# Attention finished by the sixth block, and the first matmul of three blocks as seven half products

## The chip, the core and the metric

The kernel runs on one core of a Trainium2 chip. The metric is device time in microseconds (us) for one execution. Three runs of the kernel before gave 280.96 us as their median (280.19 to 281.14). One execution was profiled; it took 281.67 us, of which the profile covers a span of 279.9 us from the first to the last instruction. The five engines of the core run in parallel, each in the order of its own queue: PE multiplies matrices, DVE and ACT do elementwise work, POOL and SP here mostly issue DMA transfers.

## What is computed

Chunked attention over 8 batches, 8 heads, 576 positions and 64 features, with chunks of 64, and behind it a two-layer block with a swish gate whose steepness is a vector. All tensors are float32; the kernel works in float16 with float32 sums.

```
scores = (q_chunk @ k_chunk.T) / 8          # every chunk of 64 positions by itself
attn   = exp(scores - max) / sum            # softmax over the chunk
x      = attn @ v_chunk                     # to 4608 tokens x 512
h      = x @ w_in                           # 512 -> 2048
g      = h * sigmoid(beta * h)              # beta: one number for each of the 2048
out    = g @ w_out                          # 2048 -> 512
```

## The kernel before

**Units and blocks.** The 4608 tokens are cut into 18 units of 256 tokens; two units make one of nine blocks (j = 0 to 8). Attention is done by unit, the two layers by block of 512 tokens.

**Attention of a unit.** `load_unit` (L120) issues six or more DMAs of q, k and v on POOL's queue, which also turn float32 into float16. From unit 8 on, `emit_T` (L147) issues two DMA transposes of a unit's k and q on SP's queue (`kT`, `qT`), and then asks for the load of the unit four further on; q and k have four buffers each, so that load can start only when the transpose of the unit that used the buffer has landed. `emit_sc` (L205) is 32 small score matmuls and an exp on ACT; `emit_pv` (L239) is 32 small value matmuls; `emit_norm` (L294) divides by the softmax sums on DVE; `emit_xt_dma` (L337) issues two more DMA transposes on SP, which bring the result (`xt`) into the layout that the first layer reads.

**First layer.** `emit_m` (L352) makes one of the 16 groups of 128 hidden features of a block: four matmuls of 128x128 on 512 columns (L359) into one PSUM tile `hps`, a tanh of half of beta times h on ACT (L367), and `emit_mg` (L345), one DVE instruction that makes (tanh + 1) * h (L347) in float16, the tile `gt`. The factor two that this leaves is taken out earlier: the sums of the softmax are made with ones of value 2.0.

**Second layer.** From block 1 on it is done as seven products of half size in place of eight (Strassen's scheme in Winograd's form): `emit_sum` (L412) makes four sums `sm` of quarters of `gt` on DVE, `emit_wt` four of the weights, once; `emit_prod` (L442) is one half of such a product, eight matmuls on 256 columns (L475). Results leave PSUM by an ACT copy (L492) and a DVE add (L495), and go out by DMA from SP (L429).

**Order.** The program is written out by hand. For each block, a list of items with a position between 0 and 1 is sorted, and all engines get their instructions in that order: the 16 groups of block j, the 14 half products of block j - 1, the four sums, and in blocks 2 to 7 the attention of the two units of block j + 1 (L637 to L642). Engines wait for each other by semaphores. PE is in order: a score matmul whose transpose has not landed holds up everything behind it on PE. SP is in order too: the transposes of `xt`, those of k and q and the stores of results share its queue.

Of the kernel before, what the change touches and what calls it, by code (L numbers as in the profile page):

```python
# [15 lines left out]
def kernel(  # L16
# [10 lines left out]
    nc = tc.nc  # L27
# [15 lines left out]
    big = ctx.enter_context(tc.tile_pool(name="big", bufs=1))  # L43
    qk_p = ctx.enter_context(tc.tile_pool(name="qk", bufs=4))
    qt_p = ctx.enter_context(tc.tile_pool(name="qt", bufs=2))
    et_p = ctx.enter_context(tc.tile_pool(name="et", bufs=3))
    rd_p = ctx.enter_context(tc.tile_pool(name="rd", bufs=2))
    x_p = ctx.enter_context(tc.tile_pool(name="x16", bufs=4))
    xt_p = ctx.enter_context(tc.tile_pool(name="xt", bufs=3))
    gt_p = ctx.enter_context(tc.tile_pool(name="gt", bufs=2))  # L50
    sg_p = ctx.enter_context(tc.tile_pool(name="sg", bufs=4))
    osb_p = ctx.enter_context(tc.tile_pool(name="osb", bufs=4))
    osl_p = ctx.enter_context(tc.tile_pool(name="osl", bufs=6))
    ps_p = ctx.enter_context(tc.tile_pool(name="ps_p", bufs=4, space=bass.MemoryType.PSUM))
    ps_s = ctx.enter_context(tc.tile_pool(name="ps_s", bufs=1, space=bass.MemoryType.PSUM))
    ps_x_open = tc.tile_pool(name="ps_x", bufs=1, space=bass.MemoryType.PSUM)
    ps_x = ps_x_open.__enter__()
    ps_y = []

# [6 lines left out]
    braw = const.tile([128, 32], FP32)  # L66
    bt = const.tile([128, 32], FP32)
    w_in16 = [big.tile([128, KDM, 256], FP16, name=f"win{g}") for g in range(8)]
    w_out16 = [big.tile([128, 4, DM], FP16, name=f"wout{g}") for g in range(4)]
    vbig = big.tile([128, NV, H, VP], FP16)  # L70
    wt = [big.tile([128, 8, 256], FP16, name=f"wt{i}") for i in range(4)]
# [3 lines left out]
    NB = len(blocks)  # L75
    XU = 8
    unit_block = {}
    for j, (u0, n) in enumerate(blocks):
# [160 lines left out]
    def emit_pv(u, halves=(0, 1)):  # L239
        et = et_t[u]  # L240
        if u >= XU:
            x = ps_s.tile([128, 2, 512], FP32, tag="s", name="x")
            y = [ps_p.tile([128, 512], FP32, tag="p", name="xe") for _ in range(2)]
            x_t[u] = (x[:, :, 0:7 * (D + 1)].rearrange("p r (n d) -> p r n d", n=7), y)
            for n in (7, 0, 1, 2, 3, 4, 5, 6):
                for r in range(2):
                    s, g = divmod(n, 4)
                    i = 2 * u + s
                    o = x_t[u][0][:, r, n] if n < 7 else y[r][:, 0:D + 1]
                    for c in range(2):  # L250
                        nc.tensor.matmul(  # L251
                            out=o[64 * c:64 * c + 64],
                            lhsT=et[64 * r:64 * r + 64, g % 2, 4 * s + 2 * c + g // 2, :],
                            rhs=vbig[64 * r:64 * r + 64, i % NV, 4 * c + g, 0:D + 1],
                        )
            return
        for s in halves:
            i = 2 * u + s
            pool, tag = (ps_x, "x") if s == 0 else (ps_s, "s")
            x = pool.tile([128, 2, 4, 128], FP32, tag=tag, name="x")  # L260
            for g in range(4):
                for r in range(2):
                    for c in range(2):
                        nc.tensor.matmul(
                            out=x[64 * c:64 * c + 64, r, g, 0:D + 1],
                            lhsT=et[64 * r:64 * r + 64, s, 4 * c + g, :],
                            rhs=vbig[64 * r:64 * r + 64, i % NV, 4 * c + g, 0:D + 1],
                        )
            x_t[u, s] = x
# [6 lines left out]
    def emit_norm_whole(u, s):  # L276
        x, y = x_t[u][0:2]
        if s == 0:
            rx = rd_p.tile([128, 2, 8, 1], FP32, tag="rx", name="rx")
            x16 = x_p.tile([128, 2, 2, 4, D], FP16, tag="x32", name="x16", bufs=2)  # L280
            for r in range(2):
                nc.vector.reciprocal(out=rx[:, r, 7], in_=y[r][:, D:D + 1])
                nc.vector.tensor_scalar(out=x16[:, 1, r, 3], in0=y[r][:, 0:D], scalar1=rx[:, r, 7], scalar2=None,
                                        op0=ALU.mult)
            nc.vector.reciprocal(out=rx[:, :, 0:7], in_=x[:, :, :, D:D + 1])
            norm_part(x16[:, 0], x[:, :, 0:4], rx[:, :, 0:4])
            x_t[u] = (x, rx, x16)
            x16_t[u, 0] = x16[:, 0]
            return
# [25 lines left out]
    def emit_xt_pe(u, s):  # L315
        xf = x16_t.pop((u, s)).rearrange("p r h d -> p (r h d)")
        xp = ps_p.tile([128, 4, 128], FP16, tag="p", name="xp")
        xt = xt_at(u, s)
# [25 lines left out]

    def emit_mg(j, m):  # L345
        c0, n, sg, hps = mg_t.pop((j, m))
        nc.vector.scalar_tensor_tensor(  # L347
            out=gt_t[j][:, m, c0:c0 + n], in0=sg[:, 0:n], scalar=1.0, in1=hps[:, 0:n],
            op0=ALU.add, op1=ALU.mult,
        )  # L350

    def emit_m(j, m, c0=0, n=None, gate=True):  # L352
        n = blocks[j][1] * UNIT if n is None else n
        if j not in gt_t:
            gt_t[j] = gt_p.tile([128, KFF, 512], FP16, tag="gt", name="gt")
        hps = ps_p.tile([128, 512], FP32, tag="p", name="hps")
        xr = xt_t[j].rearrange("p t (r k) (c q) -> p (t r) (k c) q", r=2, c=2)
        for kk in range(KDM):
# [6 lines left out]
            )  # L365
        sg = sg_p.tile([128, 512], FP32, tag="sg", name="sg")
        nc.scalar.activation(out=sg[:, 0:n], in_=hps[:, 0:n], func=ACTF.Tanh, scale=bt[:, m:m + 1])  # L367
        mg_t[j, m] = (c0, n, sg, hps)
# [5 lines left out]
    def emit_t(j, t, k0=0, k1=None):  # L374
        k1 = KFF if k1 is None else k1
        if k0 == 0:
            ops_t[j, t] = ps_p.tile([128, DM], FP32, tag="p", name="ops")
        ops = ops_t[j, t]
# [33 lines left out]
    def emit_sum(j, i, lo=0, hi=8):  # L412
# [6 lines left out]
        nc.vector.tensor_tensor(out=sm[i][:, lo:hi, :], in0=a, in1=b, op=op)  # L419

    acc_t = {}
    oq_t = {}
# [19 lines left out]
    def emit_prod(j, p, t):  # L442
        last = j == NB - 1
        if p == 1 and t == 0:
            if j == 1:
                a = [ps_p.tile([128, 512], FP32, tag="p", name="acc") for _ in range(2)]
            else:
                a = [ps_y[0].tile([128, 512], FP32, tag=n, name=n) for n in ("ya", "yb")]
            if last:
                a = [(a[i], ps_p.tile([128, 512], FP32, tag="p", name="acc")) for i in range(2)]  # L450
            acc_t[j] = a
# [47 lines left out]
    def emit_idle(n, w):  # L499
        d = ps_p.tile([128, 512], FP32, tag="p", name="warm")  # L500
        for _ in range(n):
            nc.tensor.matmul(out=d[:, 0:w], lhsT=idle[:, 0:128], rhs=idle[:, 0:w])

    with tc.manual_schedule():
# [61 lines left out]
        for s in range(4):  # L566
            for t in range(4):
# [12 lines left out]
                if s == 3 and t == 3:  # L580
                    emit_xt_unit(2)
                emit_t(0, t, 4 * s, 4 * s + 4)
        emit_sc(3, True)
        for m in range(2):
# [15 lines left out]
        def att_items(u, a0, w):  # L600
            if u >= XU:
# [5 lines left out]
                    (a0 + (0.70 if u + 1 < XU else 0.10) * w, 3, ("T", u + 1))]  # L607

        for j in range(1, NB):
            if j == 3:  # L610
                ps_x_open.__exit__(None, None, None)
                ps_y.append(ctx.enter_context(tc.tile_pool(name="ps_y", bufs=1, space=bass.MemoryType.PSUM)))
            items = []
# [6 lines left out]
            else:  # L620
                m0 = 0.36 if j == 2 else 0.02
                items += [(m0 + (1 - m0) * m / KFF, 0, ("m", m)) for m in range(KFF)]
                for i, p in enumerate((1, 2, 6, 5, 7, 3, 4)):
                    for t in range(2):
                        items.append((0.98 * (2 * i + t) / 14, 1, ("prod", p, t)))
                if j == NB - 1:
                    for i, c in ((2, 0.74), (0, 0.82), (1, 0.86), (3, 0.90)):
                        items.append((c, 4, ("pre", i)))
                for i in range(4):
                    s0 = (0.01, 0.08, 0.25, 0.33)[i] if j == 2 else 0.005 + 0.07 * i  # L630
                    items.append((s0, 4, ("sum", i)))
                if j == 2:
# [3 lines left out]
                              (0.24, 3, ("T", 6)), (0.30, 2, ("xp", 5, 0)), (0.32, 2, ("xp", 5, 1))]  # L636
                if j + 1 < NB:  # L637
                    if j == 2:
                        items += att_items(6, 0.36, 0.27) + att_items(7, 0.60, 0.27)
                    else:  # L640
                        for i in range(2):
                            items += att_items(2 * j + 2 + i, 0.03 + 0.43 * i, 0.43)  # L642
            items.sort(key=lambda it: it[:2])
            for _, _, it in items:
# [20 lines left out]
                elif it[0] == "wt":  # L665
                    emit_wt(it[1], (1,))
                elif it[0] == "Th":
                    emit_T(it[1], (it[2],))
                elif it[1] < NU:
                    emit_T(it[1])  # L670
        for i in (0, 1, 3):
            emit_sum(NB - 1, i, 4, 8)
        for p in (1, 2, 6, 5, 7, 3, 4):
            for t in range(2):
# [32 lines left out]
```

## Time and profile before

| part of the profiled execution | what it shows |
|---|---|
| whole execution, and its span | 281.67 us, 279.9 us |
| PE busy | 269.3 us, 96% of the span |
| DVE busy, ACT busy | 197.9 us, 147.7 us |
| chain that ended last, share on PE | 84% |
| blocks 3 to 7, each | 27.96 to 27.97 us |
| block 8 (no attention in it) | 26.04 us |
| last 14 half products and the end | 15.65 us |

Busy time is the sum over an engine's instructions. The chain that ended last is followed back from the last instruction, at each step to what released it, so an engine with 84% of that chain is the one that sets the time. The blocks are read as the stretches between the first half products of consecutive blocks; block 3 runs from 98.38 to 126.35 us.

### The profile page before, as it was taken

Reading aid. Unit: us, or ns where it says so; the run is one execution under the profiler, and the core shown is the slowest. Engines: PE = TensorE matmul, PEld = TensorE weight load, DVE = VectorE, ACT = ScalarE, POOL = GpSimd, SP = SyncE. Lnnn points to the kernel's source line nnn. Section 1 sums busy time; section 2 is a strip of 40 time slices with the busy share of each in tenths; the row PEclk is TensorE's granted clock in tenths of the full one; section 3 lists DMA queues with packets and bytes.
Section 4 is the critical chain, followed back from the end, with each engine's and each line's share of the span. In section 5 each row is a group of like instructions: output and inputs, shape, how many; then the busy total and the mean of one; then the engine's idle time right before and its main releaser. Section 6 shows DMA issues by size and latency. Waiting matters only on the chain.

```text
span 279.9 us, 7409 instructions
## 1 busy us (share of the span) xinstructions
PE 269.3 (96%) x3090; PEld 174.4 (62%) x3090; DVE 197.9 (71%) x357; ACT 147.7 (53%) x234; POOL 97.0 (35%) x124
## 2 busy tenths in 40 slices
PE   7589999899999999999999999999999999999995
PEld 2466445666755566666666666666666666666784
DVE  3557664699987679576957695769576957775841
ACT  3368606886655564546454645464546454544521
POOL 8864478489548805134181525000000000000000
PEclk9959999999999999999999999999999999999999
DMA  9999999999999998999999999991747114111213
GB/s 137 170 196 204 185 174 170 250 171 156 161 139 126 152 215 91 172 166 155 108 136 132 215 107 158 124 190 37 115 115 115 33 44 115 37 40 37 75 40 112
DMA packets 145952, 36.92 MB, mean 132 GB/s; under 512 B 130048, under 2 KB 145408, under 8 KB 145920
## 3 DMA queue, kind: packets, MB, share of 16 engines
q0 software_dynamic: 101216, 18.10, 83.7%
q1 hardware_dynamic: 44704, 18.37, 35.8%
q8 instruction: 24, 0.39, 0.6%
q14 instruction: 8, 0.07, 0.1%
HBM read 36.71 MB, written 9.44 MB: 165 GB/s over the span
## 4 chain that ended last, share of the span: by engine, by line
PE 84%; DVE 6%; POOL 3%; DMA 2%; ACT 2%; issue 1%; DVEq 0%; ACTq 0%; POOLq 0%
PE hps L359 40%; PE ya L475 17%; PE yb L475 12%; PE acc L475 6%; PE ops L380 5%; DVE gt L347 3%; DMA win<-in_moe_w_in_dram 2%; PE sc L214 1%; POOL vbig L115 1%; PE sc L227 1%; ACT sg L367 1%; PE xp L320 1%; PE x L251 1%; DVE x L304 1%; DVE kT L159 1%
## 5 line engine op out<-in xcount | busy, mean ns | idle before, releaser
L367 ACT ACTIVATE sg<-hps,bt 128x512 f32<-128x512 f32 (+1 forms) x158 | 101.8, 650 | 92.5 <-PE hps L359 76.9
L359 PE MATMUL hps<-xt,win 128*128 128x512 f16 (+1 forms) x632 | 145.4, 366 | 1.6 <-DMA win<-in_moe_w_in_dram 0.9
L347 DVE SCALAR_TENSOR_TENSOR gt<-sg,hps 128x512 f16<-128x512 f32 (+1 forms) x158 | 99.1, 636 | 57.5 <-ACT sg L367 57.0
L359 PEld LDWEIGHTS <-win 128*128 128x128 f16 x632 | 61.4, 99 | 44.2 <-issue 1.4
L475 PEld LDWEIGHTS <-sm 128*128 128x128 f16 x512 | 49.0, 98 | 15.3
L475 PEld LDWEIGHTS <-gt 128*128 128x128 f16 x384 | 36.9, 98 | 12.0
L115 POOL DMA_DIRECT2D vbig<-in_v_dram x40 | 34.2, 880 | 10.3 <-DMA wout<-in_moe_w_out_dram 4.3
L101 POOL DMA_DIRECT2D qu<-in_q_dram x22 | 18.6, 859 | 54.8 <-DMA qT<-qu 46.7
L475 PE MATMUL ya<-wt,sm 128*128 128x256 f16 x208 | 27.0, 273 | 0.0
L419 DVE TENSOR_TENSOR sm<-gt 128x2048 f16<-128x2048 f16 (+1 forms) x17 | 19.6, 1156 | 0.3
L101 POOL DMA_DIRECT2D ku<-in_k_dram x22 | 18.8, 881 | 0.0
L380 PE MATMUL ops<-wout,gt 128*128 128x512 f16 x64 | 14.5, 380 | 0.0
L475 PE MATMUL ya<-wout,gt 128*128 128x256 f16 x104 | 13.5, 273 | 0.0
L475 PE MATMUL yb<-wt,sm 128*128 128x256 f16 x104 | 13.5, 273 | 0.0
L475 PE MATMUL yb<-wout,gt 128*128 128x256 f16 x104 | 13.5, 273 | 0.0
L475 PE MATMUL yb<-wout,sm 128*128 128x256 f16 x104 | 13.5, 273 | 0.0
L475 PE MATMUL ya<-wt,gt 128*128 128x256 f16 x104 | 13.5, 273 | 0.0
L236 ACT ACTIVATE et<-sc 128x1024 f16<-128x1024 f32 (+1 forms) x9 | 7.3, 833 | 11.5 <-PE sc L227 11.5
L272 DVE TENSOR_TENSOR x<-x,rx 128x512 f16<-128x512 f32 (+1 forms) x20 | 12.4, 620 | 0.3
L492 ACT COPY osb<-ya 128x512 f32<-128x512 f32 x18 | 10.6, 587 | 2.4 <-PE ya L475 2.4
L304 DVE TENSOR_TENSOR x<-x,rd 128x512 f16<-128x512 f32 (+1 forms) x20 | 11.3, 583 | 0.6
L380 PEld LDWEIGHTS <-gt 128*128 128x128 f16 x64 | 6.0, 98 | 6.9
(69 smaller groups left out, 203.0 us busy)
## 6 DMA issues: line engine op xcount, KB each, us to landing
out_dram<-osb SPq DMA_DIRECT2D x32, 256.0 KB, 3.9
vbig<-in_v_dram POOLq DMA_DIRECT2D x32, 128.0 KB, 7.7
qu<-in_q_dram POOLq DMA_DIRECT2D x20, 128.0 KB, 5.7
ku<-in_k_dram POOLq DMA_DIRECT2D x20, 128.0 KB, 7.0
win<-in_moe_w_in_dram POOLq DMA_DIRECT2D x8, 256.0 KB, 9.4
wout<-in_moe_w_out_dram POOLq DMA_DIRECT2D x4, 512.0 KB, 12.8
qu<-in_q_dram POOLq DMA_DIRECT2D x4, 256.0 KB, 6.7
ku<-in_k_dram POOLq DMA_DIRECT2D x4, 256.0 KB, 6.2
```

The costliest lines, as they stand in the source:

```text
L101: nc.gpsimd.dma_start(out=tv[off:off + n, sp], in_=src[b, :, s:s + n, :].rearrange("h p d -> p h d"),)
L115: nc.gpsimd.dma_start(out=vbig[off:off + n, i % NV, :, 0:D], in_=v[b, :, s:s + n, :].rearrange("h p d -> p h d"),)
L236: nc.scalar.activation(out=et[:, s], in_=sc[:, s], func=ACTF.Exp, scale=scale)
L272: nc.vector.tensor_tensor(out=x16, in0=x[:, :, :, 0:D], in1=rd.to_broadcast(list(x16.shape)), op=ALU.mult)
L304: nc.vector.tensor_tensor(out=o, in0=x[:, r, :, 0:D], in1=rd[:, r].to_broadcast(list(o.shape)), op=ALU.mult)
L347: nc.vector.scalar_tensor_tensor(out=gt_t[j][:, m, c0:c0 + n], in0=sg[:, 0:n], scalar=1.0, in1=hps[:, 0:n], op0=ALU.add, op1=ALU.mult,)
L359: nc.tensor.matmul(out=hps[:, 0:n], lhsT=w_in16[m // 2][:, kk, (m % 2) * 128:(m % 2) * 128 + 128], rhs=xr[:, c0 // CH:(c0 + n) // CH, 2 * ...
L367: nc.scalar.activation(out=sg[:, 0:n], in_=hps[:, 0:n], func=ACTF.Tanh, scale=bt[:, m:m + 1])
L380: nc.tensor.matmul(out=ops, lhsT=gt_t[j][:, kk, t * 128:(t + 1) * 128], rhs=w_out16[kk // 4][:, kk % 4, :], start=(kk == 0), stop=(kk == K ...
L419: nc.vector.tensor_tensor(out=sm[i][:, lo:hi, :], in0=a, in1=b, op=op)
L475: nc.tensor.matmul(out=dst, lhsT=lhsT, rhs=rhs, start=(p in (1, 2, 5) and kk == 0 and (t == 0 or last)), stop=(kk == 7 and (t == 1 or last ...
L492: nc.scalar.copy(out=o, in_=acc)
```

## The change

Seven parts, all in one edit:

1. Attention is moved ahead. In block 3 three units are done (8, 9, 10), in block 4 four (11 to 14), in block 5 three (15 to 17); blocks 6 and 7 have none. `xt` gets a fourth buffer. The loads keep their rule: four units ahead.
2. From block 6 on (`QB`), groups 4 to 15 of the first layer are made in three sets of four, each as seven half products of 128x128 on 256 columns (`emit_q_prod`), 28 matmuls on 256 columns for 16 on 512. Groups 0 to 3 stay as they were.
3. The seven products need four sums of weights for each set (`emit_ws`, 12 DVE instructions, in block 6) and four differences of `xt` for each block (`emit_tx`, 4 DVE instructions).
4. The results of a set are put together by three ACT copies out of PSUM and three DVE adds into a float32 tile `hq`, and gated by six Silu instructions on ACT and four DVE scalings into `gt`. The gate in these blocks is Silu of beta times h, times 1 / beta, for groups 0 to 3 as well; before the block loop `emit_beta` makes both vectors with five small DVE instructions.
5. PSUM pools are closed and opened anew at block 6: two buffers in place of four for `hps`, two each for the new accumulators `qx` and `qz`. The SBUF of attention's tiles is given to the new tiles at position 0.70 of block 5.
6. In the normalisation of units 8 and on, two small DVE multiplications become ACT instructions with a scale.
7. In the last block the first two half products are put between the half products of the first layer, and one sum is made whole after them.

```diff
+    QB = 6
+    QM = (1, 2, 3)
...
-                nc.vector.tensor_scalar(out=x16[:, 1, r, 3], in0=y[r][:, 0:D], scalar1=rx[:, r, 7], scalar2=None,
-                                        op0=ALU.mult)
+                nc.scalar.activation(out=x16[:, 1, r, 3], in_=y[r][:, 0:D], func=ACTF.Copy, scale=rx[:, r, 7])
...
     def emit_mg(j, m):
+        if j >= QB:
+            nc.vector.tensor_scalar(out=gt_t[j][:, m, :], in0=mg_t.pop((j, m)), scalar1=rb[:, m:m + 1], scalar2=None,
+                                    op0=ALU.mult)
+            return
...
+        if j >= QB:
+            nc.scalar.activation(out=sg, in_=hps, func=ACTF.Silu, scale=bs[:, m:m + 1])
+            mg_t[j, m] = sg
+            return
...
+    def emit_ws(i, n):
...
+        in0, in1, op = ((a21, a22, ALU.add), (o[0], a11, ALU.subtract),
+                        (a11, a21, ALU.subtract), (a12, o[1], ALU.subtract))[n]
+        nc.vector.tensor_tensor(out=o[n], in0=in0, in1=in1, op=op)
...
+    def emit_tx(j, n):
...
+        in0, in1 = ((b12, b11), (b22, tx[0]), (b22, b12), (b21, tx[1]))[n]
+        nc.vector.tensor_tensor(out=tx[n], in0=in0, in1=in1, op=ALU.subtract)
...
+    def emit_q_prod(j, i, p):
+        x, z = qz_t[j, i][0:2]
+        dst = x if p in (1, 6, 7, 4) else z
...
+        for s in range(2):
+            for kk in range(2):
...
+                nc.tensor.matmul(
+                    out=dst[:, s, :], lhsT=lhsT, rhs=rhs,
+                    start=(p in (1, 2, 5) and s == 0 and kk == 0),
...
+    def emit_q(j, i, s):
...
+        for p in ((1, 2), (6, 5), (7, 3), (4,))[s]:
+            emit_q_prod(j, i, p)
+            if p in (1, 6, 5):
+                o = {1: hq[:, 0:2, 0], 6: hq[:, 0:2, 1], 5: hq[:, 2:4, 1]}[p]
+                nc.scalar.copy(out=o, in_=z if p == 5 else x)
+            if p in (2, 7, 3):
+                o = {2: hq[:, 0:2, 0], 7: hq[:, 2:4, 1], 3: hq[:, 0:2, 1]}[p]
+                nc.vector.tensor_tensor(out=o, in0=x if p == 7 else z, in1=o, op=ALU.add)
...
+    def emit_q_silu(j, i, part):
...
+        for b in (0, 1):
+            if part == 0:
+                silu(hq[:, 2 + b, 0], x[:, b], 2 + b)
+            elif part == 1:
+                silu(hq[:, b], hq[:, b], b)
+            else:
+                silu(hq[:, 2 + b, 1], hq[:, 2 + b, 1], 2 + b)
...
+    def emit_q_scale(j, i, r):
...
+            nc.vector.tensor_scalar(
+                out=gt_t[j][:, m, :], in0=hq[:, b].rearrange("p c q -> p (c q)"),
+                scalar1=rb[:, m:m + 1], scalar2=None, op0=ALU.mult)
...
+        ATT = {2: ((6, 0.36, 0.27), (7, 0.60, 0.27)),
+               3: ((8, 0.02, 0.33), (9, 0.35, 0.33), (10, 0.68, 0.32)),
+               4: ((11, 0.01, 0.25), (12, 0.26, 0.25), (13, 0.51, 0.25), (14, 0.76, 0.25)),
+               5: ((15, 0.02, 0.27), (16, 0.29, 0.27), (17, 0.56, 0.27))}
+        LANE = [(("m", 0), ("q", 1, 0), ("m", 1), ("q", 1, 1), ("q", 2, 0), ("q", 1, 2), ("q", 2, 1), ("q", 1, 3),
+                 ("q", 2, 2), ("q", 3, 0), ("q", 2, 3), ("q", 3, 1), ("m", 2), ("q", 3, 2), ("m", 3), ("q", 3, 3)),
...
-                if j + 1 < NB:
-                    if j == 2:
-                        items += att_items(6, 0.36, 0.27) + att_items(7, 0.60, 0.27)
-                    else:
-                        for i in range(2):
-                            items += att_items(2 * j + 2 + i, 0.03 + 0.43 * i, 0.43)
+                if j == QB - 1:
+                    items.append((0.70, 6, ("open",)))
+                    items += [(0.72 + 0.04 * n, 6, ("tx", QB, n)) for n in range(4)]
+                for u, a0, w in ATT.get(j, ()):
+                    items += att_items(u, a0, w)
```

## The prediction

> **What bounds the kernel now.** I read the page first (busy shares, slices, chain), then the stretches of the blocks, then the queue of SP with each transpose's landing.
>
> ```profile
> PE 269.3 (96%) x3090; PEld 174.4 (62%) x3090; DVE 197.9 (71%) x357; ACT 147.7 (53%) x234; POOL 97.0 (35%) x124
> ...
> DMA  9999999999999998999999999991747114111213
> ...
> PE 84%; DVE 6%; POOL 3%; DMA 2%; ACT 2%; issue 1%; DVEq 0%; ACTq 0%; POOLq 0%
> ```
>
> PE sets the time; the DMA engines are full until about slice 27 (189 us), which so far costs nothing. Blocks 3, 7 and 8 (columns: stretch, length, then busy time of PE, weight loads, DVE, ACT, POOL; clock, DMA share, GB/s):
>
> ```profile
> 98.38:126.35 27.97, 27.97 (x306) 18.19 (x305) 21.42 (x38) 14.94 (x22) 7.99 (x10) 1.00 1.42 161
> ...
> 210.25:238.21 27.96, 27.96 (x306) 18.18 (x305) 20.84 (x37) 14.95 (x22) 0.00 (x0) 1.00 0.37 77
> 238.21:264.25 26.04, 26.04 (x179) 17.17 (x177) 19.34 (x27) 13.34 (x20) 0.00 (x0) 1.00 0.12 41
> ```
>
> PE has no gap in any block. Block 8 is 14 half products and 16 groups; in the chain a half product is 0.87 us (eight matmuls on 256 columns, 0.109 each), so a group is (26.04 - 12.18) / 16 = 0.866. Two units of attention add 27.97 - 26.04 = 1.93: 0.48 for each step of scores or of values.
>
> **Half products (gain).** Twelve groups are 10.39 us; their 84 matmuls on 256 columns at 0.109 are 9.13. Three blocks: 3 x 1.26 = 3.8 us less, and a block of 24.8 us. Attention's PE work only moves.
>
> **Attention ahead (the cost I hold for decisive).** SP's queue around unit 10's transposes (start, length), then what POOL's next load waits for:
>
> ```profile
> 108.35 2.85 SPq L339 DMA_TRANSPOSE xt<-x  x2
> 111.25 0.57 SPq L429 DMA_DIRECT2D out_dram<-osb  x1
> 111.99 1.46 SPq L154 DMA_TRANSPOSE kT<-ku  x1
> 113.56 4.03 SPq L154 DMA_TRANSPOSE qT<-qu  x1
> ...
> 123.62 1.75 POOL L101 DMA_DIRECT2D qu<-in_q_dram  x2 [10.43 <-DMA qT<-qu]
> ```
>
> This `qT` took 9.5 us from issue to landing; with loads in flight the five from unit 10 on took 9.5, 10.0, 10.3, 9.5, 11.8; after the last load (unit 15 on) 4.2, 4.2, 3.9. Unit 8's took 6.2, issued just as a load began.
>
> In program order the transposes of unit u+1 stand on SP behind the `xt` of unit u-1. From the first value matmul of u-1 to its `xt` the trace has 4.35 us (104.00 to 108.35) or 3.2 (116.25 to 119.45); `xt` to the next instruction 2.9; a store, where one stands between, 0.74; `kT` to `qT` 1.57. So unit u+1 is ready 8.4 to 9.55 us (with a store) or 7.7 to 8.8 (without), plus the landing, after the values of u-1 begin. Before, two units were 12 to 16 us apart and this just fitted; now the pitch is about 9.6 us in block 3 and 7.5 in block 4.
>
> Laying the changed order out with 0.87, 0.866 and 0.48 from 98.38: values of unit 8 at 102.3, scores of 10 at 118.5; values of 10 at 122.5, scores of 12 at 135.2; values of 12 at 138.3, scores of 14 at 151.0. With a landing of 9.5: unit 10 is ready at 120.2 to 121.4 (1.7 to 2.9 late), unit 12 at 140.4 to 141.5 (5.2 to 6.3 late), unit 14, counted from its own stretch, 4.5 to 5.6 late. Together 11.4 to 14.8 us. With 4.2: 0 to 1.3. Odd units follow in the shade of the even ones. Unit 16 has no load beside it: ready 12.6 to 13.8 after the values of 14, scores due 12.7 after them, 0 to 1.1 late, which I leave to the bounds. By capacity instead: a load starts every 14.6 us (107.93 to 166.28 in four steps), of which some 4 us show a DMA share under 1.3 (down to 0.2) where the rest has 1.3 to 2.4; a unit's load, transposes and stores are then about 11 us of work. Five of them from 107.4, where unit 9's `qT` landed, end at 162.4, and up to 4 us of the last load may trail unit 14: 7 to 11 late at 151.0. I take 7, the low end of that and near the middle of 0 to 14.8.
>
> Behind a waiting score matmul on PE stand the half products and groups of the same block; ACT, DVE and the stores wait for those. The load of unit u+4 is late with the transpose, so the lateness doesn't build up loads but spaces them.
>
> **A stall and the clock.** The trace has one such gap (columns as above, the clock is the third from the end):
>
> ```profile
> 10.00:13.10 3.10, 1.10 (x13) 0.75 (x12) 2.38 (x6) 1.45 (x4) 3.10 (x5) 1.00 1.82 181
> 13.10:14.90 1.80, 1.56 (x72) 1.30 (x72) 0.00 (x0) 0.98 (x3) 0.73 (x2) 0.98 1.93 178
> 14.90:21.70 6.80, 6.14 (x63) 4.43 (x62) 4.03 (x12) 3.83 (x9) 3.90 (x7) 0.50 1.45 197
> ```
>
> PE was busy for 1.10 of 3.1 us and then got half the clock for 6.8, a loss of up to 3.4. Two stalls of 5 us could bring that twice, but while PE is slow the transposes catch up, so a stall's second half is partly paid already. Bounds 0 and 6.8; I take 1.7, half of one.
>
> The Trainium skill ("TensorE: Matmul & The Clock Gate", "HAM oscillation — how this bites in real kernels") speaks against this change: a gap longer than one window of about 3.4 us halves the clock, until as long a stretch of work restores it. By it the two longer stalls would cost some 1.7 each, an estimate from that page, 3.4 where I put 1.7; the row above is dearer for one gap.
>
> **DVE in the new blocks.** Adds into `hq` look like L495's (0.682, the same shape and types), sums are 1.218, `tx` and `ws` are half of L410's 0.674 and a bit, 0.41 by the slope to 1.218. The scaling (float32 in SBUF to float16, 128x512) isn't in the trace: the cast of that shape took 0.384, the gate that reads PSUM 0.683. I take 0.42, by the cast, which reads and writes the same memories. A block: 9 x 0.682 + 4 x 1.218 + 3 x 0.682 + 4 x 0.41 + 16 x 0.42 = 21.4 of 24.8 us. Block 6 has 12 `ws` more: 26.3, 1.5 over; half is made up where PE doesn't need it yet: 0.7 (0 to 1.5). At 0.683: 30.5 and 25.6, that is 5.7 + 0.8 + 0.8 = 7.3 over.
>
> **ACT in the new blocks.** Per set three copies of 0.587, two Silu on 512 and four on 256 columns, priced as tanh (0.687, 0.475), 5.0; with 4 x 0.687 and 4 x 0.587 a block has 20.2 of 24.8 us. One more table load (1.28 in the trace) is hidden in the 4.6 left; without that cover it is 1.3. Silu dearer than tanh: 0 to 1 per block, covered too.
>
> **The rest.** Two DVE multiplications of 0.284 a unit go to ACT (0.37 by the 256-column copy, an upper bound), which has 13 us free a block: nothing on the path; if ACT were full, 0.75 a unit. `tx` of block 6 waits on DVE for the last `xt` transposes (2.4 to landing, 1.2 of it behind other work): gates queue behind it, PSUM has four buffers of 0.87 and more: nothing, bound 1.2. `emit_beta` falls where DVE is idle (47 to 50 us): nothing, bound 0.9. Pools anew at block 6: nothing, bound 0.9, one group. At the end, the last half product is followed by two Silu (0.95), two scalings (0.84), two sums (1.38) and some 0.2 of handing over, 3.4, against three half products of PE work (2.6): 0.8 (0 to 1.5).
>
> **Sum.** 281.67 - 3.8 + 7 + 1.7 + 0.7 + 0.8 = 288.1. The profiled execution lies 0.71 over the median of the runs: 287.4.
>
> **Rivals.** *The transposes keep up* (the other side): SP issues them before the load they would collide with, and a `qT` of units 10, 12 and 14 lands within 6 us, as unit 8's did. For it: DMA had idle stretches before. Against: five of five were slow. Stall 0.5: 281.67 - 3.8 + 0.5 + 0.7 + 0.8 = 279.9, by the median 279.2. It decides up to about 2.3 us of stalls in all.
> *DVE becomes the bound* in blocks 6 to 8, scaling at 0.683, transposes in time: 281.67 - 3.8 + 0.5 + 7.3 + 0.8 = 286.5, 285.8 by the median. Against: the cast's row.
> *The half products don't do what they say*: each of the 21 steps a block waits for its accumulator to be copied or added, at 0.11 us, what a half product takes longer behind attention (0.98 for 0.87): 3 x 21 x 0.11 = 6.9, so 281.67 + 3.1 + 0.5 + 0.7 + 0.8 = 286.8, 286.1 by the median. For it: products 6, 5, 7, 3 and 4 all read after a copy or an add. Against: 2.6 us lie between the steps of a set, a copy and an add are 1.3.
>
> **Chances.** Forecast 0.56, transposes keep up 0.28, DVE 0.08, half products 0.08. A measurement here can tell 0.3%, 0.84 us: faster is under 280.1, slower over 281.8. Of the 0.28, 0.25 are faster and 0.03 same; of the forecast 0.04 are same and 0.02 faster (stalls of 2 us); the others are slower. Faster 0.27, same 0.07, slower 0.66. Range: low end the second case less a little, 278.4; high end 294.0, stalls of 11.4 and the clock at 3.4 (281.67 - 3.8 + 11.4 + 3.4 + 1.5 - 0.71 = 293.5). The likeliest case alone has 282 to 294.
>
> **What would show it.** Right: PE waits at L214's scores for `qT` in blocks 3 and 4, chiefly for units 12 and 14, landings of 8 us and over there, blocks 3 to 5 longer than 28.9, 29.9 and 28.9 us, perhaps a clock under 1.00 behind them; blocks 6 to 8 near 25 us. Wrong: blocks 3 to 5 at those lengths with no such wait; or blocks 6 to 8 over 27.

## The result, and the profile after

The changed kernel takes 295.77 us (median of four runs, 295.46 to 295.98) where the kernel before, run beside it, takes 280.85: a ratio of 1.0534, with a 95% interval from 1.0513 to 1.0555. The forecast was 287.4 us with a range up to 294.0: slower as foretold, but by 14.9 us instead of 6.6, and outside the range. The profiled execution took 295.46 us, with a span of 293.7. Ratios here and below leave out a run that took over 1.5% longer than the fastest of its kernel; medians and ranges are of all runs.

The page of the changed kernel, in the lines that were read before: busy time, the granted clock and the DMA engines in 40 slices (7.3 us each), and the chain of waits by engine.

```profile
PE 272.5 (93%) x3198; PEld 186.9 (64%) x3198; DVE 209.1 (71%) x392; ACT 168.0 (57%) x300; POOL 97.0 (33%) x124
...
PEclk9899999999999999799799599999999999999999
DMA  9999999999999999999999966714102011110223
...
PE 64%; DMA 13%; DVE 8%; POOL 5%; ACT 3%; issue 3%; SPq 2%; POOLq 0%; ACTq 0%
```

DMA had 2% of the chain and has 13%. The clock row has three notches (slices 17, 20 and 23) that were not there. They come right behind three waits of PE:

```profile
PE sc L216 <- DMA qT<-qu: 10.4, 3, 3.8
```

That is 10.4 us in three waits, the longest 3.8, all of score matmuls for `qT`. The stretches of these waits and of the work behind each show the two halves of the loss, waiting and a lower clock (columns: stretch, length, then busy time of PE, weight loads, DVE, ACT, POOL; clock, DMA share, GB/s). The last two rows are blocks 6 and 7.

```profile
117.20:120.75 3.55, 0.01 (x3) 0.04 (x2) 1.06 (x2) 0.69 (x1) 0.00 (x0) 1.00 1.37 143
120.75:125.40 4.65, 4.65 (x48) 2.55 (x49) 0.69 (x1) 1.71 (x2) 4.25 (x5) 0.63 1.28 206
...
139.18:142.19 3.01, 0.01 (x2) 0.04 (x2) 3.01 (x4) 0.00 (x0) 0.00 (x0) 1.00 1.13 162
142.19:146.00 3.81, 3.81 (x45) 2.26 (x46) 0.78 (x2) 1.71 (x2) 3.42 (x4) 0.55 0.96 148
...
159.67:163.51 3.84, 0.00 (x0) 0.03 (x1) 0.69 (x1) 0.69 (x1) 0.00 (x0) 0.90 1.75 157
163.51:169.50 5.99, 5.99 (x64) 3.56 (x68) 1.38 (x2) 1.71 (x2) 0.00 (x0) 0.50 1.19 176
...
200.60:226.30 25.70, 25.70 (x218) 21.13 (x216) 23.79 (x46) 17.48 (x32) 0.00 (x0) 1.00 0.14 47
226.30:251.50 25.20, 25.02 (x214) 20.75 (x212) 20.48 (x36) 17.71 (x36) 0.00 (x0) 1.00 0.13 42
```

PE stands for 3.55, 3.01 and 3.84 us, ahead of units 10, 12 and 14; behind each wait it has about half the clock (0.63, 0.55 and 0.50 as the mean of the stretch), which costs 4.65 x 0.37 + 3.81 x 0.45 + 5.99 x 0.50 = 1.7 + 1.7 + 3.0 = 6.4 us. Together 16.8. Blocks 6 and 7 took 25.7 and 25.2 us where 24.8 was forecast.

SP's queue in front of the third wait (start, length of the issue):

```profile
149.48 2.50 SPq L340 DMA_TRANSPOSE xt<-x  x2
152.16 2.46 SPq L156 DMA_TRANSPOSE kT<-ku  x1
154.72 2.35 SPq L156 DMA_TRANSPOSE qT<-qu  x1
```

Unit 12's scores ended at 142.8, its `xt` transposes could be issued at 149.48, unit 14's transposes behind them, and `qT` landed at 163.4, 8.7 us after its issue: 21.4 us from one even unit to the next, where PE had work for 16 (15.8 between the same scores in the run without late loads, below). Unit 17's load was issued from 151.6 to 156.9, into this landing. That suggests two causes, both named in the prediction: the order on SP, and DMA engines that can't move five loads so soon. The experiments take them apart.

### The profile page after: what moved, and what is told of

It is laid out like the page before. It is cut to its first block, busy times and chain, and to the rows that moved or that the text cites. A ratio compares the mean times of both kernels' runs of the same rounds, so it can differ in the third digit from the quotient of the medians.

```text
span 293.7 us, 7739 instructions
## 1 busy us (share of the span) xinstructions
PE 272.5 (93%) x3198; PEld 186.9 (64%) x3198; DVE 209.1 (71%) x392; ACT 168.0 (57%) x300; POOL 97.0 (33%) x124
## 2 busy tenths in 40 slices
DMA packets 145955, 36.95 MB, mean 126 GB/s; under 512 B 130048, under 2 KB 145408, under 8 KB 145920
## 4 chain that ended last, share of the span: by engine, by line
PE 64%; DMA 13%; DVE 8%; POOL 5%; ACT 3%; issue 3%; SPq 2%; POOLq 0%; ACTq 0%
PE hps L364 21%; PE ya L577 12%; PE yb L577 10%; DMA qT<-qu 7%; PE acc L577 5%; PE qx L477 4%; PE qz L477 4%; PE ops L389 4%; DMA qu<-in_q_dram 3%; DMA ku<-in_k_dram 2%; DVE gt L352 2%; POOL vbig L117 2%; ACT hq L505 2%; DVE gt L519 1%; SPq L156 1%
## 5 line engine op out<-in xcount | busy, mean ns | idle before, releaser
L364 PE MATMUL hps<-xt,win 128*128 128x512 f16 (+1 forms) x488 | 110.1, 363 | 1.0 <-ACT xt L325 0.6
L352 DVE SCALAR_TENSOR_TENSOR gt<-sg,hps 128x512 f16<-128x512 f32 (+1 forms) x110 | 67.0, 616 | 45.6 <-ACT sg L376 44.9
L376 ACT ACTIVATE sg<-hps,bt 128x512 f32<-128x512 f32 (+1 forms) x110 | 69.0, 634 | 44.0 <-PE hps L364 43.6
L364 PEld LDWEIGHTS <-win 128*128 128x128 f16 x488 | 47.0, 99 | 34.4 <-issue 3.4
L577 PEld LDWEIGHTS <-gt 128*128 128x128 f16 x384 | 37.3, 99 | 11.3 <-DVE gt L519 1.1
L519 DVE TENSOR_SCALAR gt<-hq,rb 128x512 f16<-128x512 f32 x36 | 15.9, 481 | 7.7 <-ACT hq L505 6.9
L505 ACT ACTIVATE hq<-hq,bs 128x256 f32<-128x256 f32 (+1 forms) x36 | 19.2, 613 | 0.0
L222 ACT ACTIVATE et<-sc 128x1024 f16<-128x1024 f32 x10 | 10.2, 1021 | 12.3 <-PE sc L216 12.3
L477 PEld LDWEIGHTS <-ws 128*128 128x128 f16 x144 | 14.1, 98 | 2.3 <-issue 0.7
L216 PE MATMUL sc<-qT,kT 64*64 64x64 f16 x320 | 4.8, 203 | 10.4 <-DMA qT<-qu 10.4
L495 ACT COPY hq<-qx 128x512 f32<-128x512 f32 x18 | 10.6, 587 | 5.8 <-PE qx L477 5.8
```

Source lines behind the costliest of these rows:

```text
L352: nc.vector.scalar_tensor_tensor(out=gt_t[j][:, m, c0:c0 + n], in0=sg[:, 0:n], scalar=1.0, in1=hps[:, 0:n], op0=ALU.add, op1=ALU.mult,)
L364: nc.tensor.matmul(out=hps[:, 0:n], lhsT=w_in16[m // 2][:, kk, (m % 2) * 128:(m % 2) * 128 + 128], rhs=xr[:, c0 // CH:(c0 + n) // CH, 2 * ...
L477: nc.tensor.matmul(out=dst[:, s, :], lhsT=lhsT, rhs=rhs, start=(p in (1, 2, 5) and s == 0 and kk == 0), stop=(s == 1 and kk == 1), skip_gr ...
L495: nc.scalar.copy(out=o, in_=z if p == 5 else x)
L505: nc.scalar.activation(out=o, in_=src, func=ACTF.Silu, scale=bs[:, m:m + 1])
L519: nc.vector.tensor_scalar(out=gt_t[j][:, m, :], in0=hq[:, b].rearrange("p c q -> p (c q)"), scalar1=rb[:, m:m + 1], scalar2=None, op0=ALU. ...
```

## The experiments

Ratios are against the kernel before, run beside them on the same chip. Its median was 280.42 us beside the first four runs (attention alone, transposes first, no late loads, 16 matmuls on zeros at three places), 281.32 beside the next four (no late v, half the packets, 30 matmuls on zeros, the first slower pace) and 280.65 beside the last four. Differences from the changed kernel's 295.77 cross these rounds, so some 0.5 us of them is uncertain.

**The attention ahead alone.** The kernel before with `xt` bufs 4 and

```
-   items += att_items(2 * j + 2 + i, 0.03 + 0.43 * i, 0.43)
+   for u, a0, w in ATT.get(j, ()):
+       items += att_items(u, a0, w)
```

> The kernel before, with only the attention of units 8 to 17 moved ahead into blocks 3 to 5 (and a fourth xt buffer); no half products, tanh gate throughout. Theory (stalls on the transposes and the half clock behind them are the whole loss): the three gaps of after (3.55, 3.01, 3.84 us) and the clock lost behind them (4.65 x 0.37, 3.81 x 0.45 and 5.99 x 0.50 = 6.4 us) come back here, 16.8 us: 280.9 + 16.8 = about 297.5 us. Rival (part of the loss comes from the second part of the change, its pools and its tail): 285 to 294 us.

297.43 us (296.2 to 298.99), ratio 1.0607 (1.056 to 1.0655). PE waits at the scores of the same units, for 3.4, 2.7 and 4.2 us. The whole loss is in the moved attention. Against this run the rest of the change wins 1.7 us by the medians, 2.1 by the ratios.

**Transposes first on SP.** In `att_items`, for units from 8 on:

```
-   (a0 + 0.10 * w, 3, ("T", u + 1))
+   (a0, 3, ("T", u + 2))
```

(unit 9's transposes come directly behind unit 8's, in block 2).

> The changed kernel, with the q and k transposes of unit u+2 emitted right after the scores of unit u, so that on SP's queue they stand ahead of the xt transposes of unit u instead of behind those of unit u+1's predecessor. Theory (SP's order makes them late; 10 us of landing is then in the shade): qT of units 10, 12 and 14 is issued 9 us or more sooner, no gap of PE over 1 us in blocks 3 to 5, clock 1.00, about 278 to 280 us. Rival (capacity of the DMA engines: loads, transposes and stores of a unit are 11 us of work and the pitch of block 4 is 7.5): landings grow over 12 us, gaps stay at units 13 and 14, 287 to 293 us.

289.9 us (289.37 to 290.98), ratio 1.0349 (1.0317 to 1.038): 5.9 us come back, 9 to 11 don't. This is nearer the rival's case: its time and its waits came, its landings of over 12 us did not. About 1.5 of the rest are of this run's own making: the first groups of block 3 wait 1.3 us, which a later run without unit 9's early transposes does not show. Lines of the transposes from 100 us on (issue time min/median/max in ns, then from issue to landing in us):

```profile
L156 SPq DMA_TRANSPOSE kT<-ku x8: 1242/2654/3730, 101.1 to 176.5; - x8
L156 SPq DMA_TRANSPOSE qT<-qu x8: 1375/2929/3871, 102.4 to 177.9; - x8
...
DMA to landing us min/median/max: 4.4/9.5/10.8
```

`qT` of units 10, 12 and 14 was issued 6.6 to 8.7 us sooner than in the changed kernel (9 expected), but half of the transposes take 9.5 us and more to land, and SP itself is held 2.7 to 2.9 us by an issue. Its queue is nearly full: from 110.4 to 171.4 us its issues take 58.0 of 61.0 us. Four that follow each other:

```profile
144.59 3.45 SPq L156 DMA_TRANSPOSE kT<-ku  x1
148.14 2.23 SPq L156 DMA_TRANSPOSE qT<-qu  x1
150.47 0.54 SPq L531 DMA_DIRECT2D out_dram<-osb  x1
151.10 4.64 SPq L340 DMA_TRANSPOSE xt<-x  x2
```

Waits of 2.4, 2.0, 2.0 and 0.3 us remain at units 13 to 16, and from unit 12 to 15 scores come 11.2, 10.9 and 10.0 us apart: about the pace that the prediction's "11 us of work" for a unit allows. Whether the engines set it directly, or by holding SP's issues, this run doesn't separate.

**No late loads.** In the loads of a unit, where `held` keeps each unit's q and k tiles (`load_v` is left out for these units too, so they compute on older data and give another output):

```
+   if u >= 13:
+       q_t[u], k_t[u] = held[u - 4]
+       held[u] = held[u - 4]
+       return
```

> The changed kernel without the loads of q, k and v for units 13 to 17 (these units compute on data of units loaded before, so the output of those rows is another); every transpose stays. Theory (a transpose lands late because casting loads are in flight): qT lands in about 4 us from unit 10 on, and as SP's order then leaves 0 to 1.3 us of lateness, gaps are under 1.5 us in all, 278 to 280 us. Rival (the order on SP alone makes them late, landing hardly matters): gaps of 2 us and more stay at units 12 and 14, 286 us and over.

279.48 us (278.5 to 280.53), ratio 0.9959 (0.9937 to 0.9981). No score matmul waits any more, with SP's order as in the changed kernel. The transposes from 100 us on:

```profile
L165 SPq DMA_TRANSPOSE qT<-qu x9: 1244/1322/4130, 96.1 to 166.6; - x9
L165 SPq DMA_TRANSPOSE kT<-ku x8: 1232/1269/1291, 108.7 to 165.3; - x8
...
DMA to landing us min/median/max: 3.1/3.3/11.2
```

They land in 3.3 us (median) instead of 9.5, with issues of 1.3 instead of 2.7 to 2.9. The cleaner comparison is with the changed kernel, which has the same order on SP: there `qT` of units 10 to 14 landed in 10.7, 3.3, 8.3, 7.4 and 8.7 us, here in 3.1 or 3.2. (The 11.2 is unit 9's, with unit 12's load still beside it.) So a transpose is slow because loads are in flight beside it. That agrees with the Trainium skill ("DMA: Bandwidth & Descriptors", "SWDGE vs HWDGE vs iDMA"): GpSimd's and SP's transfers share the same 16 engines, which take turns between their queues.

This run also gives the schedule that the changed kernel would have had without the waits. The exponentials of units 10, 12 and 14, which start as the scores end, in the changed kernel:

```profile
121.25 1.02 ACT L222 ACTIVATE et<-sc 128x1024 f16<-128x1024 f32 x1 [3.25 <-PE sc L216]
...
142.84 1.02 ACT L222 ACTIVATE et<-sc 128x1024 f16<-128x1024 f32 x1 [3.75 <-PE sc L216]
...
164.20 1.02 ACT L222 ACTIVATE et<-sc 128x1024 f16<-128x1024 f32 x1 [3.75 <-PE sc L216]
```

and without late loads:

```profile
118.19 1.02 ACT L231 ACTIVATE et<-sc 128x1024 f16<-128x1024 f32 x1
...
134.63 1.02 ACT L231 ACTIVATE et<-sc 128x1024 f16<-128x1024 f32 x1 [0.53 <-PE sc L225]
...
150.69 1.02 ACT L231 ACTIVATE et<-sc 128x1024 f16<-128x1024 f32 x1
```

Its unit 8 came 0.3 us later than the changed kernel's (99.71 and 99.41), so the lateness is 121.25 - 117.9 = 3.4 us at unit 10, 142.84 - 134.3 = 8.5 at unit 12, 164.20 - 150.4 = 13.8 at unit 14. With the 3.0 us of half clock behind unit 14 that is 16.8; the two profiled executions differ by 295.46 - 279.09 = 16.4.

**A third of the late loads less.** `load_v` only for units under 13 (the later ones use older values of v and give another output).

> The changed kernel without the loads of v for units 13 to 17 (a third of the late loads in bytes and in packets; these units use older values, so the output of those rows is another). What is left open by the runs so far: with the transposes moved ahead on SP, units 13 to 16 still came 10.0 to 11.2 us apart, as they did in the changed kernel (21.5 us for two). Theory C (capacity: about 11 us of DMA work a unit, some 7 of it loads): a unit takes about 8.7 us, the scores of unit 14 are 4 to 6 us late instead of 13.5, 284 to 288 us. Rival (fixed latency: a transpose behind any load lands in about 9 us): the gaps stay as they were, 293 us and over.

283.82 us (282.21 to 285.35), ratio 1.0109 (1.0044 to 1.0175), a little under the capacity theory's range. The profiled run, one of the faster two of four (282.42), has waits at units 10, 12 and 13 of 2.0, 1.0 and 1.1 us, the clock at 1.00 throughout, 17.2 us from unit 12 to 14 (8.6 a unit, 8.7 expected) and unit 14's scores 4.2 us late (4 to 6 expected). The transposes' median landing is 5.0 us, so a fixed landing time is out.

**The same bytes in half the packets.** The loads of q and k for units from 13 on by the form that the first eight units use:

```
-   if u >= XU:
+   if XU <= u < 13:
```

> The changed kernel with the loads of q and k for units 13 to 17 in rows of two heads' positions, 512 bytes each instead of 256: the same bytes, half the packets, so a third less of all late packets (the rows stand in another order, so the output of those rows is another). If the packets are what costs: like the run without v, 284 to 288 us. If the bytes are: as the changed kernel, 294 to 297 us.

293.41 us (291.06 to 296.37), ratio 1.0407 (1.0328 to 1.0486), waits of 3.1, 4.0 and 4.0 us. The median is just under the 294 to 297 us that the bytes theory expected and far over the 284 to 288 of the packets. All packets of the execution fell from 145,955 to 135,587, as many as without v (135,539). Of the 12 us that the run without v won, 2.4 are seen by the medians and 3.6 by the ratios (1.3 to 5.9 with both intervals). So the number of packets explains half of it at most; that the bytes are the rest is argued by elimination, not shown by a run of its own.

**PE kept busy.** To see what the lower clock costs by itself, PE was given matmuls on zeros to do ahead of a unit's scores, in place of the wait:

```
+   if it[1] in (10, 12, 14):
+       emit_idle(16, 512)
    emit_sc(it[1])
```

> The changed kernel with 16 matmuls on zeros (512 columns, 3.5 us in all) put on PE ahead of the scores of units 10, 12 and 14, so that PE does not idle while it waits for qT. Theory A (half clock behind a gap is a loss of its own, 6.4 us): clock 1.00 through blocks 3 to 5, 295.8 - 6.4 = about 289.4 us. Theory B (the slow stretch was partly paid already, since the transposes caught up during it): the next wait grows by what the clock gives back, 292 to 295 us.

297.15 us (294.27 to 299.57), ratio 1.056 (1.0498 to 1.0622), that is 1.056 x 280.42 = 296.1 us: over both ranges, no gain. But PE still waited 0.9, 2.3 and 1.9 us and the clock fell behind the last two, so the run decides nothing. With 30 matmuls at each place:

> As the run with 16 matmuls on zeros before the scores of units 10, 12 and 14, with 30 of them (6.5 us), since behind 16 PE still idled 0.9, 2.3 and 1.9 us and the clock fell twice. Theory B (the DMA engines set the pace, the half clock was paid within the wait): no gap, clock 1.00, and still 293 to 298 us. Theory A (the half clock is a loss of its own): about 289.4 us.

298.57 us (298.01 to 298.64), ratio 1.0614 (1.0583 to 1.0645), no wait, clock 1.00 in all three blocks. It decides nothing either: no wait was left because the zeros took longer than the waits had. So each place was tried with about its own gap:

> The changed kernel with 16 and 14 matmuls on zeros (3.5 and 3.0 us) before the scores of units 10 and 12 alone. Theory B (DMA engines set the pace up to unit 14): the waits of units 12 and 14 grow by about what the clock gives back (3.4 us), 295 to 298 us. Theory A (half clock a loss of its own): 295.8 - 3.4 = about 292.4 us.

296.63 us (293.78 to 297.77), ratio 1.0541 (1.0497 to 1.0585). PE's waits from 95 us to block 6, in the fastest of the six runs (293.78), which is the one that was profiled:

```profile
141.75 0.45 PE L216 MATMUL sc<-qT,kT 64*64 64x64 f16 x32 [1.19 <-DMA qT<-qu]
163.26 0.64 PE L216 MATMUL sc<-qT,kT 64*64 64x64 f16 x32 [5.63 <-DMA qT<-qu]
```

The clock was 1.00 behind units 10 and 12, and the scores of 12 and 14 began at 141.75 and 163.26, as in the changed kernel (142.19 and 163.51): what the clock gave back, the next wait took. The wait at 14 is 5.6 us instead of 3.8. (That this profiled execution is 1.7 us under the changed kernel's fits the clock behind unit 14, which fell for a shorter time: 0.76 over 6.24 us instead of 0.50 over 5.99.)

> The changed kernel with 17 matmuls on zeros (3.7 us) before the scores of unit 14 alone, where the last of the three gaps is (3.85 us) and no wait comes behind it. Both theories expect a clock of 1.00 behind unit 14. Theory B (the half clock behind the gaps of units 10 and 12 was paid within the next wait; the one behind unit 14, 3.0 us, was not): 295.8 - 3.0 = about 292.8 us. If the half clock costs nothing at all: 295 us and over.

293.7 us (292.3 to 296.1), ratio 1.0455 (1.0415 to 1.0494): 2.1 us under the changed kernel by the medians, 2.2 by the ratios, 3.0 expected. The zeros fill the gap and the clock stays up:

```profile
163.00:170.00 7.00, 6.87 (x105) 4.32 (x104) 3.41 (x8) 3.42 (x6) 0.00 (x0) 1.00 1.42 184
```

In this kernel, then, half a clock costs time of its own only behind the last wait.

**A slower pace.** Half products from block 7 (`QB = 7`), transposes first, and

```
+   3: ((8, 0.02, 0.33), (9, 0.38, 0.33), (10, 0.74, 0.33)),
+   4: ((11, 0.10, 0.33), (12, 0.46, 0.33), (13, 0.82, 0.33)),
+   5: ((14, 0.18, 0.33), (15, 0.54, 0.33), (16, 0.86, 0.33)),
+   6: ((17, 0.26, 0.33),)
```

> Half products from block 7 on only (two blocks instead of three), attention of units 8 to 17 spread evenly to the middle of block 6, one unit every 0.36 of a block (10.3 us), and the transposes of unit u+2 right behind the scores of unit u. Theory C (capacity of 11 us a unit, reached only from unit 13 on): no gap over 1.5 us, 2/3 of what the half products give, 279 to 280.5 us. Rival (pitch still under the capacity): gaps of 1 us and more at three units, 282 to 285 us.

284.08 us (282.64 to 284.57), ratio 1.0094 (1.0062 to 1.0126): in the rival's range, but not by its way. No score waits; the first groups of block 3 wait 2.04 us, with a clock of 0.54 over the 3.5 us behind. Unit 9's transposes, which wait for their load, stood ahead of unit 7's `xt`. With them behind it (`a0 + 0.56 * w` in unit 7's items):

> As the run with half products from block 7 on, but unit 9's transposes stand behind unit 7's xt on SP, as in the kernel before (ahead of them they made the first groups of block 3 wait 2.04 us, with half a clock of 1.6 us behind). Expected if that was the only loss: 284.1 - 3.6 = 280.5 us, about as the kernel before or a little under it (279.5 to 281). Rival (a pitch of 10.3 us a unit leaves waits as soon as the first transposes start later): gaps at two units or more, 282 us and over.

279.94 us (279.23 to 281.45), ratio 0.998 (0.9958 to 1.0003). No wait over 0.3 us from block 3 on, although the transposes still land in 9.5 us (median): the landing is hidden. It is the fastest version here with the right output, and it can't be told apart from the kernel before. The same pace with SP's old order:

> Half products from block 7 on, attention spread as in the two other runs of this kind, but SP's order as in the changed kernel (transposes of unit u+1 behind the xt of unit u-1). If the DMA engines' capacity alone counts: no gap, 280 to 281.5 us. If the way from the scores of u over its xt to the scores of u+2 (21.4 us for two units in the changed kernel, against 20.6 here) counts as well: small gaps at units 12, 14 and 16, 281.5 to 285 us.

286.01 us (283.33 to 291.59), ratio 1.0135 (1.0088 to 1.0183), that is 1.0135 x 280.65 = 284.4 us for the four of seven runs that the ratio keeps: at 10.3 us a unit, SP's order decides over some 4.5 us. Only the slowest run was profiled, so where the four lose their time is not seen.

## Why the prediction was off

**The step that failed** is "7 to 11 late at 151.0. I take 7, the low end of that and near the middle of 0 to 14.8." It had worked out the lateness at unit 14 in two ways, along SP's order (11.4 to 14.8) and by what the DMA engines can move (7 to 11), and then took the lesser as if they were two opinions on one number. They are two conditions, and the scores need both: the later one sets the time. The trace has 13.8 us, inside the span that the order gave. Unit by unit the lateness grew by 3.4, 5.1 and 5.3 us at units 10, 12 and 14, where the order's reckoning had 1.7 to 2.9, 5.2 to 6.3 and 4.5 to 5.6; only the first is off by more than 0.1. The runs show each condition. With the order mended, some 6 us at unit 14 stay (its exponential at 158.3 against 150.7, 1.5 of it there since unit 8), and 289.9 us; with the pace eased to 10.3 us and the old order, 284.4; with both mended no wait; and without late loads the same order costs nothing, since the order's reckoning has the slow landing in it.

How good the capacity number was stays open. Five units' work was to end at 162.4, and unit 14's `qT` landed at 163.4, but that landing followed from SP's order (issue at 154.72, 8.7 us to land), so the agreement may be luck. In the run with transposes first the loads also began sooner (unit 13's at 98.5 us instead of 106.2), so its 6 us don't measure the engines alone either. Nor is it shown whether taking off "up to 4 us" for the last load was wrong: unit 17's load was issued beside unit 14's transposes in both runs (from 151.6 us in the changed kernel, from 148.7 in the other).

**The clock**, 1.7 us with bounds 0 to 6.8, measured 6.4. That "a stall's second half is partly paid already" was right: the runs with matmuls on zeros at some of the places show that the 3.4 us behind units 10 and 12 were in the next waits, and that those behind unit 14 were a loss of their own (3.0 by the clock, 2.1 won back). Counted so, lateness at unit 14 and the clock behind it, the sum is 281.67 - 3.8 + 13.8 + 3.0 + 0.7 + 0.8 = 296.2 for a profiled 295.46. The high end of the range had 11.4 and 3.4 in it, not the upper bounds that the text itself gave (14.8 and 6.8).

**The half products** were to win 3.8 us and give 1.5 back. From unit 8's scores to PE's last work the run without late loads is 1.6 us shorter than the profile of before, not 2.3. Blocks 6 and 7 took 25.7 and 25.2 us for 24.8; PE was busy through the whole of block 6, so its 0.9 us are no wait, and where they come from stays open. DVE was dearer than put, the scaling 0.481 us for 0.42 (`tx` and `ws` 0.42 for 0.41, the adds 0.683 as read), but had room: it was busy 23.8 of block 6's 25.7 us, and PE waited for it twice for 0.2 us and once, in the tail, for 0.3. The two rivals that put the bound in DVE or in the steps of the half products are out by these short waits. The rival with transposes that keep up fell with the landings: 10.7, 8.3 and 8.7 us at units 10, 12 and 14 where it needed 6.

What it named to look for was there: waits at the scores for `qT` at units 10, 12 and 14, landings of 8 us and over, the lower clock, and blocks 6 and 7 near 25 us.

## What to carry to other kernels

Where an operand comes late by the order of a queue and also by the capacity of the engines behind it, work out both arrival times and take the later; the lesser is no cautious middle. DMA engines that were full at no cost yet had no slack here: the change asked for the same bytes sooner and paid for it. So write down the transfers' own pace (here 11 us a unit) before compressing their users to 7.5. And a clock that falls behind a wait was, here, a loss of its own only where no further wait for the same supply followed.

## What was not expected of the hardware

Waits of 2.0 to 3.0 us could be enough to halve the clock. Two waits of nearly one length in the run with transposes first (columns as above; each wait, then the work behind it):

```profile
144.40:146.87 2.47, 0.10 (x1) 0.03 (x1) 0.69 (x1) 0.69 (x1) 1.50 (x2) 1.00 1.90 187
146.87:150.40 3.53, 3.53 (x44) 1.94 (x44) 0.00 (x0) 1.02 (x1) 2.94 (x4) 0.55 1.57 169
155.50:157.67 2.17, 0.14 (x1) 0.03 (x1) 0.78 (x2) 0.69 (x1) 1.27 (x2) 1.00 1.53 196
157.67:161.20 3.53, 3.53 (x84) 2.60 (x84) 0.98 (x2) 1.71 (x2) 0.88 (x1) 1.00 1.67 167
```

2.4 us brought the clock to 0.55, 2.0 us left it at 1.00. Over all runs, in blocks 3 to 5, two of five waits of 1.9 to 2.0 us lowered the clock behind them (to 0.54 and 0.64), every wait of 2.3 us or more did, and none of 1.3 or less. The Trainium skill ("TensorE: Matmul & The Clock Gate", "HAM oscillation — how this bites in real kernels") puts the limit at some 3.4 us; the measurement goes before it.

A DMA transpose's issue is held too: 1.3 us on SP without late loads, 2.7 to 2.9 with them in the run with transposes first. Everything behind it on SP comes later by that, stores and `xt` among it.
